# The first loads of a planned attention-and-MLP kernel: slot 0 through the hardware queue, slot 1 cast on chip, decay powers on Pool, and a new plan

## The chip, the cores and the metric

The kernel runs on one core of a Trainium2 chip. Its time is the device time in microseconds of one execution; lower is better. Three runs of the kernel before gave 208.41, 208.84 and 209.43 us, median 208.84. The profile is that of one execution; its times are in us from the start of its span, and an instruction carries the line of the kernel before, such as L614. Engines: PE is TensorE, PEld its weight loads, DVE is VectorE, ACT is ScalarE, POOL is GpSimd, SP is SyncE, which here only issues transfers.

## The reference

Inputs are q, k, v of shape (4, 8, 768, 64) in f32 (batch, heads, time, head dimension) and two MLP weights, `w_in` (512 x 2048) and `w_out` (2048 x 512).

```python
gamma = 1.0 - 2.0 ** (-5.0 - np.arange(H))
for t in range(S):
    state = gamma * state + einsum('bhd,bhe->bhde', k[:, :, t], v[:, :, t])
    y[:, :, t] = scale * einsum('bhd,bhde->bhe', q[:, :, t], state)
# y, transposed to (B*S, H*D), is x
h = x @ w_in
out = (h * np.cos(h)) @ w_out
```

The first part is a recurrent attention with one decay per head; the second is an MLP whose activation is h cos h.

## The kernel before

**Tiles.** Time is cut into chunks of 128, and two batches go together, so there are 12 *slots* (two batch pairs of six chunks). `ORDER` takes the first chunk of both pairs first, so that slots 0 and 1 need no carried state. A slot has 256 rows of x (two batches of 128). Two slots make a *group* of 512 rows, on which the MLP works.

**Steps of a slot p**, by the names that the planner gives them (u and b are halves):

- loads of q, k, v (`load`, L284 to L300), 512 KB of f32 each;
- `cq`, `ck`, `cv`: conversion to bf16 in SBUF (`conv_q`, `conv_k`, `conv_v`). From slot 2 on q and v are multiplied by powers of the decay (`gq`, `gk`) on the way. In slots 0 and 1 the decay lies in the masks `dec` instead, so q and k are only cast, and `rv` makes an undecayed bf16 copy of v (`raw_v`);
- `tq`, `tk` (or `t`): transposes on TensorE (L364), evicted by `eq`, `ek` (L316 on ACT, L318 on DVE). Slots 6 and up are transposed by DMA instead (`dt`, L353);
- `a`: scores (L402 in slots 0 and 1, L392 later), multiplied by the mask in `m` (L411, DVE). For two tiles, one each in slots 0 and 1, ACT saves the scores (`ms`, L419) and Pool multiplies them (`ml`, L423);
- `y`: the output of the slot (L434 in slots 0 and 1, `y_block` with L483, L497, L511 later), and `s`: the state update; `yc` writes y as bf16 into `xt`, the transposed x of the group; `sc` copies the state.

**Steps of the MLP.** A unit of 128 columns of w_in: `f` for a whole group (L593: four matmuls of 512 rows), or `h` for one slot and two column blocks at once (L614: eight matmuls of 256 rows, so that the first slot can start before its neighbour is there). Each is followed by `cos` (L601, ACT) and `mul` (L605 or L622, DVE) into `gt`. `o` is a quarter of an output block (L638), `oc` its copy out of PSUM and its store. h0.0 is the first half unit, on slot 0 with column blocks 0 and 1.

**Order.** The schedule is manual. The opening and the first two groups (slots 0 to 5, and the transposes and scores of slot 6) are ordered by `Plan`: every step has engines, a cost, the steps it comes after, a rank and tokens that it takes (PSUM banks, `cos` buffers, DMA semaphores, one `port` for DVE and Pool steps that read SBUF). `Plan.run` walks through time and gives each free engine its lowest-ranked step that is ready; `SHIFT` changes the ranks of named steps and `ON` their engines. Only the order is kept: each engine executes its list strictly in order, with waits on semaphores for real dependencies. Where TensorE has nothing ready early on, the planner puts in *fillers* (`idle_mm`, L667), matmuls of zeros; seven more stand ahead of the plan. From group 2 on, the order is written out in a loop (the last one of the kernel): there one `f` unit and one `o` part alternate. It begins with `o_mm(1, 0, 0)` and `f_mm(2, 0)`.

**Loads.** Pool issues the software queue in the order of `LOADS`, at most eight in flight: after a first casting load of slot 0's k ("K", f32 in HBM, bf16 in SBUF) come "Q1" and "K1", q and k of slot 1, also cast by the transfer, into `qs` and `kx`; then v0, v1 (f32), and w_in in pieces cast to bf16: w0A (column block 0), w0B (block 1), w0b (2 and 3), w1a, w1b, w2 and so on, with later slots and w_out (`o0` to `o3`) between. SP issues q of slot 0 in two halves ahead of everything (`q0`, `q1` in the call at the start stand for the two batches, not for slots).

Of the kernel before, what the change touches and what calls it, by code (L numbers as in the profile page):

```python
# [28 lines left out]
class Plan:  # L29
# [35 lines left out]
    def run(self, start, cold_until=0.0, look=0.0, fill=None, hold=""):  # L65
# [6 lines left out]
        t = 0.0  # L72
        while left:
            nxt = []
            for e in "SPADE":
# [6 lines left out]
                for op in left:  # L82
# [12 lines left out]
                    for k, n in op["take"]:  # L95
                        tk = sorted(self.tokens[k])
                        n += op["spare"] if k == "bank" else 0
                        if len(tk) < n:
                            ok = False
                            continue  # L100

                        at = max(tk[n - 1] - 0.5, tk[n - 3]) if n > 5 else tk[n - 1]
                        if at > t + 1e-9:
                            nxt.append(at)
                            ok = False
# [33 lines left out]
                for k, n in op["take"]:  # L139
                    self.tokens[k].sort()  # L140
                    del self.tokens[k][:n]
                op.update(eng=e, start=t, free=t + busy, done=t + took, lat=self.LAT[e])
                free[e] = t + busy
                if op["mb"]:
                    self.dma = max(self.dma, t + busy + 1.6) + op["mb"] / op["rate"] + op["lag"]
                    op.update(done=self.dma + 0.9, lat=0.0)
                for k, n in op["give"]:
                    self.tokens[k] += [op["done"] + 0.052] * n
# [18 lines left out]
HOLD = ""  # L167
SHIFT = {"ml010": 25.5, "mulf0.2": -74.7, "f0.3": 0.3, "cosf0.2": -11.6, "cosf0.3": -2.2, "mulf0.3": -4.9, "f0.2": 2.8, "m011": -20.0, "mulh1.4": -20.5, "m000": 82.7, "cosf0.5": -41.6, "ck21": 45.1, "a31": -124.5, "m100": 2.2, "f0.5": 23.0, "a5": -2.5, "v0": -97.2, "ms110": 6.4, "ml110": -41.8, "cosf0.4": -0.9, "f0.4": -9.8, "mulf0.5": 16.9, "eq51": 13.1, "m110": 64.4, "t20": -21.1, "k5": -46.0, "mulf0.8": 31.6, "yc21": -50.4, "f0.6": 2.1, "f0.7": 55.3, "ek10": -92.1, "w0b": -22.2, "a21": -34.2, "h1.0": 81.4, "cosh2.2": 3.0, "m501": 38.5, "yc30": -23.3, "ml011": -27.8, "mulf0.15": 5.8, "sc5": 79.1, "m201": -81.3, "mulh2.2": -18.0, "oc1": -45.8, "mulf0.14": -66.8, "cq31": -32.2, "mulf0.9": -47.9, "mulf0.6": 5.7, "cosf0.7": -27.8, "a30": -8.1, "cosf0.6": -7.2, "h0.2": -12.1, "eq21": -4.6, "cq51": 3.2, "cq41": 38.6, "f0.14": 23.8, "ek20": -13.4, "yc50": 39.8, "cv51": 23.4, "ek51": 88.5, "mulh2.10": 23.3, "cq70": 8.6, "f0.10": -46.0, "mulf0.13": 1.5, "h1.6": 5.9, "ml100": 20.1, "f0.15": 60.8, "o2.1": -8.1, "h3.10": 31.9, "t51": 14.8, "h3.0": -7.1, "h3.14": 28.8, "cq00": -2.7, "m601": 4.7, "h1.4": 1.8, "eq11": 37.0, "cosf0.12": -60.7, "v6": -26.4, "m400": 17.7, "mulh3.12": 67.0, "w2": 49.4, "sw": -53.6, "cv10": -0.0, "rv00": 14.5, "mulh2.8": 4.5, "ek50": 72.2, "cosf0.11": 2.4, "m101": -34.4, "h2.2": 1.1, "q2": -22.9, "q5": -59.7, "cosh3.14": 19.9, "y3": 19.8, "t40": 30.7, "o2": -0.8, "mulh3.4": -0.3, "cq40": -13.2, "mulh0.2": -29.3, "y5": -35.7, "mulh3.14": -25.5, "h2.12": -50.9, "oc0": -94.2, "a10": 39.9, "ek11": -35.3, "h0.6": 6.9, "eq40": -6.2, "h2.6": 58.1, "rv10": -9.1, "dt71": -1.3, "cosh3.8": -31.0, "cosh0.2": 18.8, "cv70": -67.6, "o3.1": -13.8, "cq60": -11.1, "ck60": 71.1, "m511": 10.9, "sc4": -15.9, "o1.3": -16.8, "m510": 4.5, "k4": 12.5, "h0.4": -9.2, "cq71": 3.6, "mulh3.2": 58.9, "cosh1.2": -26.7, "mulh3.6": -1.4, "cv61": 13.7, "o2.2": -9.8, "q6": -7.4, "o0.2": -7.5, "mulh2.4": 44.5, "mulh2.6": 22.6, "mulh3.10": 16.6, "v5": -53.7, "cq61": 27.8, "o1.1": -27.2, "ck61": 0.2, "m200": -10.8, "cosf0.9": 6.3, "cosh0.4": 11.6, "q4": 78.9, "cosh3.6": -6.8, "h1.2": -87.9, "tq01": 1.8, "oc3": -74.8, "mulh0.0": -16.9, "eq01": 11.2, "t21": 6.2, "ck41": 29.7, "cosh3.4": 9.3, "oc2": 8.6, "m211": 23.9, "cq01": -56.9, "w0a": 17.8, "o1.0": -7.7, "yc01": 2.2, "k7": 54.8, "yc51": -0.7, "cosf0.13": -14.9, "cosh2.10": -36.4, "yc00": 7.1, "cosh1.4": -13.4, "ek00": -8.7, "m611": -13.9, "tk10": -101.4, "mulh0.4": -40.7, "mulf0.10": 15.2, "m600": -35.2, "a00": -17.4, "cosh2.0": -5.5, "m301": 18.6, "rv11": -50.0, "sc0": -52.0, "ek01": -31.6, "cv01": 13.3, "ek21": -3.2, "cosf0.10": 7.2, "v7": -2.1, "ek40": 18.1, "t31": 22.7, "mulh1.6": 0.2, "eq30": -9.4, "y4": 19.2, "tk11": 1.9, "ek31": -26.9, "w3b": 23.5, "cosh2.12": -0.2, "cosh0.6": 4.7, "cosh2.8": -4.4, "cosh3.2": 25.8, "cv60": 2.7, "cosh2.4": -14.4, "v4": -1.1, "mulh2.12": 36.6, "dt61": -8.8, "eq41": -12.5, "mulf0.11": 31.8, "ek41": -0.8, "eq50": 9.1, "a11": -23.9, "yc10": 9.3, "o0.3": 0.3, "dt60": -3.3, "o3.3": 50.5, "mulh2.14": -42.3, "m610": -12.1, "f0.11": -0.6, "s0": 3.1, "cv11": 38.9, "h3.8": -17.4, "yc40": 14.3, "m410": -8.4, "h2.8": -4.0, "m300": 15.8, "o0": -14.6, "cv31": -27.4, "rv01": 0.6, "cosf0.14": 2.4, "cosh2.6": 11.7, "cv50": -6.8, "m010": -1.2, "ms011": -12.0, "f0.13": -5.2, "l8": 5.1, "ck70": 3.2, "t41": 1.0, "o1.2": -2.3, "cv71": 0.5, "tq11": 31.2, "h2.4": -3.6, "mulh0.6": 8.8, "t50": 7.1, "ck31": 42.7, "yc20": -52.3, "m001": -4.7, "y01": 62.0, "y2": 15.3, "f0.12": 20.5, "ms111": 2.0, "mulh1.2": -13.9, "cosh3.10": -49.0, "ck51": -9.0, "h0.0": -0.1, "eq31": 1.4, "eq20": -5.1, "q7": 1.5, "cosh3.0": 6.2, "cosh3.12": 1.5, "cv40": 2.3, "y11": 3.6, "o1": -24.4, "cv00": -1.4, "sc2": -3.2, "m411": 18.0, "m210": -8.1, "v3": 0.0, "eq10": 1.1, "tk01": 22.8, "yc41": -25.6, "cq21": -1.8, "f0.9": -31.4}
ON = {"cv70": "P", "cv00": "D", "cv30": "D", "cv31": "D", "cv60": "D", "cv11": "D", "cv10": "P", "rv01": "D", "sc5": "D", "rv11": "A", "yc20": "D", "sc3": "D", "eq40": "DA", "eq50": "A", "rv00": "A", "yc00": "D", "yc31": "DA", "ek51": "D", "ek11": "DA", "sc4": "D", "ek20": "A", "cv61": "P", "eq01": "DA", "cv51": "D", "ek41": "D", "eq41": "A", "cv20": "P", "yc01": "DA", "eq20": "A", "eq30": "DA", "ek50": "D", "ek00": "D", "sc2": "DA", "yc50": "DA", "yc40": "A", "yc21": "A", "cq21": "D", "ek40": "DA", "cv01": "D", "cv71": "P", "cv21": "P", "ek21": "DA", "cv41": "P", "cq20": "D", "ek10": "DA", "yc30": "A", "ek01": "D"}
# [4 lines left out]
def kernel(  # L174
# [170 lines left out]
    def conv_k(p, b, e):  # L345
        copy(e, kb(p)[:, b], kf[p % PRE][:, b])
# [332 lines left out]
    load(nc.sync, 0, "q0 q1")  # L679
    load(nc.gpsimd, 0, "K")  # L680
# [320 lines left out]
```

## Time and profile before

| what | value |
|---|---|
| median of 3 runs | 208.84 us (208.41 to 209.43) |
| profiled execution | span 206.6 us, from its first to its last instruction; the page has no other time of it |
| median less span | 2.24 us |
| PE busy | 201.9 us, 98% of the span |
| PEld, DVE, ACT, POOL busy | 108.9, 112.9, 115.1, 75.2 us |
| fillers (L667) | 35, 11.2 us busy, the last at 17.29 us |
| granted TensorE clock | 9 of 10 or more in all 40 slices |
| software queue | 15408 packets, 15.47 MB |
| hardware queue | 44080 packets, 16.28 MB |

How to read it: a matmul is pipelined, so that PE can be shown busy all the time without being at its peak. What counts is in which order and from when the real matmuls follow one another. The chain that ended last tells which waits decided; the timeline of the opening tells what each first matmul waited for. The start and the length of a transfer's row are those of its issue; "to landing" is the time from the start of the issue until its semaphore.

### The profile page before, as it was taken

The numbers are of one execution on the slowest core, as the hardware profiler recorded it, in microseconds if no ns is written. First come the engines' busy times: TensorE is split into PE (matmuls) and PEld (weight loads), VectorE is DVE, ScalarE is ACT, GpSimd is POOL, SyncE is SP. The second block draws the span as 40 slices with busy tenths as digits, with TensorE's granted clock in tenths as the row PEclk, the third lists the DMA queues.
The fourth block names the chain that finished last, engine by engine and source line by source line (L and its number), as shares of the span: only waits on it lengthen the run. The fifth ranks groups of instructions, "written<-read, shape, count | busy, mean of one in ns | idle before, by whom it ended". The sixth has DMA issues, their size and how long they took to land.

```text
span 206.6 us, 5235 instructions
## 1 busy us (share of the span) xinstructions
PE 201.9 (98%) x2179; PEld 108.9 (53%) x2179; DVE 112.9 (55%) x194; ACT 115.1 (56%) x193; POOL 75.2 (36%) x79
## 2 busy tenths in 40 slices
PE   7999999999999999999999999999999999999994
PEld 2547665868945545445445445445444444444442
DVE  5477899776787548338438438448442444444000
ACT  7566794859965357547547546554555553554120
POOL 8899989799985003305206105200000000000000
PEclk9999999999999999999999999999999999999999
DMA  6999999999999865886876975501101101110212
GB/s 117 172 264 201 304 242 322 252 333 278 341 332 190 199 156 150 206 210 155 190 183 157 144 198 147 156 0 56 53 1 51 51 3 51 51 51 0 105 52 102
DMA packets 59656, 32.15 MB, mean 156 GB/s; under 512 B 48752, under 2 KB 54128, under 8 KB 59632
## 3 DMA queue, kind: packets, MB, share of 16 engines
q0 software_dynamic: 15408, 15.47, 34.6%
q1 hardware_dynamic: 44080, 16.28, 31.7%
q8 instruction: 17, 0.28, 0.6%
q10 hardware_dynamic: 144, 0.07, 0.1%
q14 instruction: 7, 0.06, 0.1%
HBM read 27.26 MB, written 6.29 MB: 162 GB/s over the span
## 4 chain that ended last, share of the span: by engine, by line
PE 93%; DMA 4%; POOL 1%; issue 0%; DVE 0%; POOLq 0%; DVEq 0%
PE bank L638 39%; PE bank L593 30%; PE bank L614 10%; DMA kx<-in_k_dram 4%; PE bank L392 2%; PE bank L483 2%; PE bank L364 2%; PE bank L658 2%; PE st_ps L511 2%; PE bank L667 2%; PE bank L497 1%; POOL ks L284 1%; PE bank L434 1%; POOL qs L284 1%; PE bank L402 0%
## 5 line engine op out<-in xcount | busy, mean ns | idle before, releaser
L601 ACT ACTIVATE cosb<-bank,halfpi 128x512 bf16<-128x512 f32 x96 | 65.6, 689 | 54.1 <-PE bank L593 47.8
L638 PE MATMUL bank<-w_out_sb,gt 128*128 128x512 bf16 x368 | 91.0, 379 | 0.0
L605 DVE TENSOR_TENSOR gt<-bank,cosb 128x512 bf16<-128x512 f32 x72 | 49.1, 689 | 55.7 <-ACT cosb L601 55.7
L593 PE MATMUL bank<-xt,w_in_sb 128*128 128x512 bf16 x288 | 73.2, 379 | 0.0
L638 PEld LDWEIGHTS <-gt 128*128 128x128 bf16 x368 | 35.5, 98 | 42.3 <-DMA w_out_sb<-in_moe_w_out_dram 0.3
L593 PEld LDWEIGHTS <-w_in_sb 128*128 128x128 bf16 x288 | 27.5, 98 | 32.3
L327 POOL TENSOR_TENSOR qs<-qf,gq 128x512 bf16<-128x512 f32 x18 | 18.5, 1046 | 42.4 <-PE bank L483 32.0
L411 DVE TENSOR_TENSOR am<-bank,mask 128x512 bf16<-128x512 f32 x40 | 24.8, 681 | 3.5 <-PE bank L392 3.5
L316 ACT COPY ob<-bank 128x512 f32<-128x512 f32 (+1 forms) x24 | 14.0, 582 | 16.0 <-PE bank L638 13.9
L614 PE MATMUL bank<-xt,w_in_sb 128*128 128x256 bf16 x192 | 22.4, 273 | 0.0
L614 PEld LDWEIGHTS <-w_in_sb 128*128 128x128 bf16 x192 | 18.6, 98 | 3.3 <-DVE xt L318 0.3
L622 DVE TENSOR_TENSOR gt<-bank,cosb 128x512 bf16<-128x512 f32 x24 | 16.2, 689 | 5.6 <-ACT cosb L601 5.4
L316 ACT CAST xt<-bank 128x512 bf16<-128x512 f32 x21 | 11.4, 588 | 10.6 <-PE bank L483 10.5
L316 ACT CAST ks<-kf 128x512 bf16<-128x512 f32 x20 | 11.5, 623 | 1.9 <-DMA kf<-in_k_dram 1.9
L667 PE MATMUL bank<-zero 128*128 128x512 bf16 x35 | 11.2, 449 | 1.1 <-DVE halfpi L683 1.1
L483 PE MATMUL bank<-am,vs 64*64 64x128 bf16 (+1 forms) x320 | 10.3, 206 | 0.1
L334 POOL TENSOR_TENSOR vs<-vf,gk 128x512 bf16<-128x512 f32 x8 | 8.2, 1043 | 6.0 <-DMA vf<-in_v_dram 3.8
L284 POOL DMA_DIRECT2D vf<-in_v_dram x8 | 9.4, 1178 | 1.9 <-DVE vs L339 1.4
L339 POOL TENSOR_TENSOR vs<-vf,gk 128x512 bf16<-128x512 f32 x8 | 8.7, 1096 | 2.5 <-PE bank L483 1.3
L318 DVE CAST stb<-st_ps 128x512 bf16<-128x512 f32 x9 | 6.2, 689 | 3.4 <-PE st_ps L511 2.6
L483 PEld LDWEIGHTS <-vs 64*64 64x64 bf16 x320 | 7.8, 107 | 0.5 <-POOLq L531 0.2
L392 PE MATMUL bank<-qkt 64*64 64x128 bf16 (+1 forms) x320 | 7.9, 206 | 0.0
(66 smaller groups left out, 131.7 us busy)
## 6 DMA issues: line engine op xcount, KB each, us to landing
out_dram<-ob SPq DMA_DIRECT2D x23, 256.0 KB, 2.5
vf<-in_v_dram POOLq DMA_DIRECT2D x8, 512.0 KB, 11.7
qf<-in_q_dram POOLq DMA_DIRECT2D x6, 512.0 KB, 12.3
kf<-in_k_dram POOLq DMA_DIRECT2D x6, 512.0 KB, 12.1
w_out_sb<-in_moe_w_out_dram POOLq DMA_DIRECT2D x4, 512.0 KB, 14.1
qf<-in_q_dram SPq DMA_DIRECT2D x4, 512.0 KB, 4.8
w_in_sb<-in_moe_w_in_dram POOLq DMA_DIRECT2D x5, 256.0 KB, 8.5
kf<-in_k_dram SPq DMA_DIRECT2D x16, 64.0 KB, 3.1
```

What stands on the lines that cost most here:

```text
L284: eng.dma_start(out=t.rearrange("p b h d -> p (b h) d"), in_=src[ds(2 * bp, 2), :, ds(c * C, C), :].rearrange("b h t d -> t (b h) d"))
L316: nc.scalar.copy(out=out, in_=in_)
L327: ENG[e].tensor_tensor(out=qb(p)[:, b], in0=qf[p % PRE][:, b], in1=bc(gq, ORDER[p] % NC), op=ALU.mult)
L411: nc.vector.tensor_tensor(out=am[p % 2][b][u], in0=bank.rearrange("p (a t) -> p a t", a=HP), in1=(dec[:, b] if p < 2 else mask[second(p, 0 ...
L483: m = nc.tensor.matmul(held["yp", p][b][ts(j, 64), a, lo:], lhsT=vs[p % NB][ts(r, 64), b, h, :], rhs=am[p % 2][b][h // 4][ts(r, 64), h % 4 ...
L593: nc.tensor.matmul(bank, lhsT=w_in_sb[:, i, ts(f, 128)], rhs=xt[g % 2][:, i, :], start=(i == 0), stop=(i == KIN - 1))
L601: nc.scalar.activation(out=cb, in_=bank, func=AF.Sin, bias=halfpi)
L605: nc.vector.tensor_tensor(out=gt[g % 2][:, f, :], in0=bank, in1=cb, op=ALU.mult)
L614: nc.tensor.matmul(bank[:, ts(e, 256)], lhsT=w_in_sb[:, i, ts(f + e, 128)], rhs=xt[g % 2][:, i, ts(hf, 256)], start=(i == 0 and e == 0), s ...
L622: nc.vector.tensor_tensor(out=gt[g % 2][:, f : f + 2, ts(hf, 256)], in0=bank.rearrange("p (f t) -> p f t", f=2), in1=cb.rearrange("p (f t) ...
L638: nc.tensor.matmul(bank, lhsT=gt[g % 2][:, f, ts(j, 128)], rhs=w_out_sb[:, f, :], start=(f == 0), stop=(f == KOUT - 1))
L667: nc.tensor.matmul(bank[:, : 256 * n].rearrange("p (n t) -> p n t", n=n), lhsT=zero[:, :128], rhs=zero.unsqueeze(1).to_broadcast([128, n, ...
```

## The change

- SP loads q and k of slot 0, each as two halves, in the order q, k, q, k. The casting load of slot 0's k on Pool's queue goes.
- Slot 0's k is therefore f32 in SBUF and is cast by a `ck` step. Slot 1's q and k ("q1", "k1" in `LOADS`) are loaded as f32 into `qf` and `kf` and cast by `cq` and `ck` steps, on DVE or ACT.
- The eight products that make `lgp` (the exponents of the decay powers) move from DVE to Pool; behind them Pool fills `ob[3]` with zeros and copies it to `ob[2]`. Both are output buffers that are overwritten before their first use. All of this stands ahead of Pool's first load.
- In `Plan`, a step on ACT no longer takes the `port` token; the rates, delays and starting times that the planner reckons with are others; `yc` of slots 0 and 1 and `rv` may go to DVE or ACT.
- `SHIFT` and `ON` are new, so the order of nearly all steps of the plan is another. Fillers in the plan: 24 where there were 28. Instructions: 190 rows of DVE where there were 185, 179 of ACT (175), 73 of Pool (70).

```diff
-    load(nc.sync, 0, "q0 q1")
-    load(nc.gpsimd, 0, "K")
+    load(nc.sync, 0, "q0 k0 q1 k1")
...
     for h in range(H):
-        nc.vector.tensor_scalar(out=lgp[:, :, h], in0=pos, scalar1=float(lg[h]),
+        nc.gpsimd.tensor_scalar(out=lgp[:, :, h], in0=pos, scalar1=float(lg[h]),
                                 scalar2=None, op0=ALU.mult)
+    nc.gpsimd.memset(ob[3], 0.0)
+    for i in range(1):
+        nc.gpsimd.tensor_copy(out=ob[2 - i], in_=ob[3])
...
-    LOADS = ["Q1", "K1", "v0", "v1", "w0A", "w0B", "w0b", "w1a", "w1b", "w2", "q2", ...]
+    LOADS = ["q1", "k1", "v0", "v1", "w0A", "w0B", "w0b", "w1a", "w1b", "w2", "q2", ...]
...
-            if p == 1:
-                T["cq", p, b], T["ck", p, b] = ld["q", p, b], ld["k", p, b]
+            if p == 1 and "Q1" in LOADS:
+                T["cq", p, b] = ld["q", p, b]
             else:
-                T["cq", p, b] = add("D" if p < 2 else CQ if p < 3 else "P", SB2 if p < 2 else TT,
+                T["cq", p, b] = add("DAP" if p < 2 else CQ if p < 3 else "P", SB3 if p < 2 else TT,
...
-            if p == 0:
+            if p == 1 and "K1" in LOADS:
                 T["ck", p, b] = ld["k", p, b]
-            elif p > 1:
-                T["ck", p, b] = add("A", SB2, lambda e, p=p, b=b: conv_k(p, b, e),
+            else:
+                T["ck", p, b] = add("DAP" if p < 2 else "A", SB3, lambda e, p=p, b=b: conv_k(p, b, e),
...
-            T["yc", p, b] = add("A", PS, lambda e, p=p, b=b: y_copy(p, b, e),
+            T["yc", p, b] = add("DA" if p < 2 else "A", PS, lambda e, p=p, b=b: y_copy(p, b, e),
...
                 for k, n in op["take"]:
+                    if k == "port" and e == "A":
+                        continue
```

The order that comes out of it at the places that matter (compiled, without times):

```
PE before:   ... tk10 tk11 3 fillers a11 a10 2 fillers y01 y00 7 fillers h0.0 y10 y11 filler h0.2 s0 h1.2 h0.4 h1.4
PE changed:  ... tk11 filler tk10 filler a11 filler y00 y01 a10 3 fillers h0.0 y10 y11 filler h0.2 h1.2 h1.4 s0
end before:  ... o3.1 o3.2 y5 o3.3 | o_mm(1,0,0) f_mm(2,0)
end changed: ... o2.2 o3.3 o2.3 y5 | o_mm(1,0,0) f_mm(2,0)
ACT changed: ... cq01 ck01 ek00 ek01 eq11 ms011 ck11 ck10 ek11 rv00 ms111 yc00 yc01 rv11 cosh0.0
DVE changed: cq00 ck00 eq00 eq01 cq11 m010 cq10 m001 eq10 m000 ek10 rv01 m101 rv10 m110 m100 cv01 yc11
POOL changed: lgp x8, fill, copy, q1 k1 v0 v1 w0A w0B w0b ml011 w1a w1b w2 ml111 q2 k2 w3a v2
```

## The prediction

> **What bounds the kernel now.** I read the page first (busy time, then the chain that ended last), then the chain in order of time, then the timeline of the opening.
>
> ```profile
> span 206.6 us, 5235 instructions
> PE 201.9 (98%) x2179; PEld 108.9 (53%) x2179; DVE 112.9 (55%) x194; ACT 115.1 (56%) x193; POOL 75.2 (36%) x79
> PE 93%; DMA 4%; POOL 1%; issue 0%; DVE 0%; POOLq 0%; DVEq 0%
> ```
>
> TensorE holds 93% of the chain; what is left lies at the start. In order of time (start, length, what):
>
> ```profile
> 1.42 1.37 POOL ks L284
> 2.79 1.13 POOL qs L284
> 3.93 7.40 DMA kx<-in_k_dram
> 14.30 1.62 PE bank L667 x7
> 15.91 0.87 PE bank L614 x8
> ...
> 69.69 1.83 PE bank L638 x8
> 71.52 1.73 PE bank L593 x8
> ```
>
> The chain begins with Pool issuing three casting loads, goes through the landing of slot 1's k at 3.93 + 7.40 = 11.33, through fillers (L667), and from 15.9 stays on real matmuls. The timeline shows what the first real one had waited for:
>
> ```profile
> 4.74 0.60 DVE L318 CAST qs<-qf 128x512 bf16<-128x512 f32 x1 [0.51 <-DMA qf<-in_q_dram]
> 5.06 2.35 POOL L284 DMA_DIRECT2D vf<-in_v_dram  x2
> 7.35 2.31 POOL L303 DMA_DIRECT2D w_in_sb<-in_moe_w_in_dram  x3
> ...
> 12.97 0.62 ACT L316 CAST gt<-vf 128x512 bf16<-128x512 f32 x1 [0.58 <-DMA vf<-in_v_dram]
> 13.66 0.64 PE L434 MATMUL bank<-am,gt 128*64 128x128 bf16 x16
> 14.11 0.59 ACT L316 CAST xt<-bank 128x512 bf16<-128x512 f32 x1
> 14.23 1.69 PE L667 MATMUL bank<-zero 128*128 128x512 bf16 x7
> 14.51 0.68 DVE L318 CAST xt<-bank 128x512 bf16<-128x512 f32 x1
> 15.75 1.04 PE L614 MATMUL bank<-xt,w_in_sb 128*128 128x256 bf16 x8
> ```
>
> h0.0 (L614) starts at 15.75. Its xt is ready at 15.19; w0A landed at 7.35 + 7.9 = 15.25 and w0B at 8.10 + 7.8 = 15.9 (their rows of issue to landing). Those follow v0 in one software stream, and v0's landing (5.06 + 7.9 = 12.95) is what the casts at 12.97 waited for. From 15.75 to the first unit of the hand-written part (L593 at 71.36) pass 55.6 us. The work in it: 24 half units at 0.873, 8 full at 0.864, 17 output parts at 0.864, 8 transpose groups at 0.44, three score groups at 0.57, y blocks 2 x 1.33 + 2 x 1.48, and 1.15 for y10, y11, s0 and one filler: 54.5. So 1.1 us are waits and switches, and the stage is a block that slides with its start. After 71.36 the code is unchanged: 135.2 us.
>
> **The change part by part.**
> *Hardware queue.* Slot 0's q halves, issued at 0.74 and 1.27, landed at 3.77 and 4.72: 0.95 us per half. With q0 k0 q1 k1 the landings are about 3.8, 4.7, 5.7, 6.6 (k landed at 1.42 + 6.3 = 7.7). SP issues two DMAs more, at 0.55 each, before its next one (L901 at 5.22): 1.1 us in an idle queue. k needs two casts more, on DVE (0.43) and ScalarE (0.6), q's second half one on ScalarE instead of DVE. ScalarE is bound there by its table load and sine, until 6.71; then two casts to 7.9, transposes to 8.4, and scores near 8.8, where L402 stands now (8.78). Nothing won or lost.
>
> *Pool's head.* One casting load goes; ahead of the first load come eight products for the decay powers, a fill and a copy, each of 128x512 f32 for the latter two. Pool's iotas end at 1.16. The eight products: 0.67 on DVE today; Pool's iotas are 0.13 to 0.15 each, so 0.67 to 1.2; I take 0.8. Fill and copy: a cast of that shape is 0.43 on DVE, a two-input product on Pool 1.04; so 0.86 to 2.1 together, and I take 1.0, nearer to the low end, since neither reads two tensors. The first software load (q1) is thus issued at 3.0, between 2.7 and 4.5, where Q1 was issued at 2.79.
>
> *The stream.* K, issued at 1.42, landed 6.3 later; in the windows from 5 to 9 us the chip moved 134 to 154 GB/s of cast output, and 347 to 353 from 10 to 12 us in f32. K, Q and K1 landed at 7.7, 9.4, 11.3 (1.8 apart), v0 and v1 1.6 apart, w0A and w0B 0.7. An issue takes 1.17. Afterwards q1 begins to flow some 2.4 after its issue starts, at 5.4, but has the hardware queue beside it until about 6.0; its 1.6 of transfer and 1.2 to the semaphore give 8.6 (without sharing 8.2; at an issue of 4.5, 9.7). Then k1 10.2, v0 11.8, v1 13.4, w0A 14.05, w0B 14.8, w0b 16.1: each 1.1 to 1.2 earlier than now. The queue gains one cast load (1.8) and 0.2 on each of two; it loses 0.9 to the later start.
>
> By the Trainium skill, SBUF — State Buffer, § SBUF: two separate sides, a VectorE copy in a two-port mode locks GpSimd out of writing descriptors. The casts at 3.80 and 4.74 lay beside the issues of 2.79 to 5.06, which kept 1.17 each, and the second cast took 0.60 instead of 0.43: here VectorE paid. By the rule q1's issue would lose 0.43 for each of two casts, and the sum 0.9 of its gain; by the rows nothing.
>
> *Casts of slot 1.* Four new ones (ck11, ck10 on ScalarE, cq11, cq10 on DVE) stand between landing and transposes. q1 is early: hidden. k1 lands at 10.2: ck11 to 10.8, ck10 to 11.4, tk11 beside it, ek11 (ScalarE) to 12.0, then rv00 to 12.6 (v0 came at 11.8). DVE's ek10 and rv01 end by 12.8. So the y matmuls run 12.7 to 13.3 (13.66 to 14.3 now). ms111 is ahead of both yc on ScalarE: to 13.2; yc00 to 13.75, yc01 to 14.3 (both on ScalarE now, 0.55 apart; today one is on DVE). a10 and three fillers end at 14.2. xt at 14.3, w0A at 14.05, w0B needed at 14.9: h0.0 at 14.45, 1.3 earlier. The casts cost 0.6 after k1, covered by waiting for v0; if v0 came earlier, they would be the path.
>
> *Behind h0.0.* The same matmuls in another order. y11 needs ml111, a Pool product behind ten loads and ml011: four issues of 1.17 and six of 0.76 from 3.0, with ml011 (1.27, held to 10.35 by ms011) among them, put it at 13.9 to 15.2 (14.16 to 15.4 now), needed at 15.6. Pool's issue order is late by 0.2 to 0.7, hidden as loads land 8 us after issue. w0b at 16.1, needed at 16.2; w1a 17.9, needed 18.0: no slack, they go with the stream. The wait for o0 ahead of o1.0 and its neighbours (L638, 0.28 of idle PEld) goes with an earlier stream: 0.15 won.
>
> *The end of the stage.* Today o3.3 stands after y5; in the change y5 is the last planned matmul, and only o_mm(1,0,0), 0.87, lies between it and the first full unit, which needs both yc5. Today ScalarE casts them at 69.73 for 1.07, just behind y5's end at 69.69. So the unit waits 0.04 + 1.07 + 0.1 - 0.87 = 0.34. This is a new wait; o3.3 hid it.
>
> *Edits of one answer.* Four fillers fewer, all ahead of h0.0, and the planner's numbers cost nothing by themselves; the clock was 1.00 in every window.
>
> Sum: -1.3 - 0.15 + 0.34 = -1.1 us: span 205.5. The page has no time of the profiled execution but its span; 2.24 lie between it and the median of 208.84 (runs 208.41 to 209.43), and I leave these as they are: 207.7.
>
> **The rivals.**
> *The gain is mostly eaten* (0 to 1 us, 208.3). If Pool's first load is issued at 3.6 to 4.0, or the three ScalarE steps ahead of yc run 0.3 late, h0.0 starts at 15.0 to 15.5. For it: the bounds of Pool's new work, and no slack at w0b and w1a. Against it: the k1 path alone would not reach beyond 14.9.
>
> *Slower: Pool's head starts the stream too late.* The landings move one for one with q1's issue. Gain is zero at an issue of 4.1; beyond 5.2 the kernel is slower by 0.5%. That needs the eight products, the fill and the copy to take 4 us in place of 1.8, and gives, at 5.5, w0B at 17.3, h0.0 at 16.95: 1.2 + 0.2 later, 210.2. For it: Pool's K issue, beside DVE's start-up work, took 1.37 in place of 1.17, and that work is still beside it. Against it: even at the upper bounds the issue is at 4.5.
>
> *A first use that stalls.* Three kinds of Pool instruction run for the first time ahead of the first load. Pool's first product (L423 at 10.18) took 1.27 and its second (14.16) 1.27 as well: a first call cost nothing there. Should one of the new kinds stall for 5 us, q1 would be issued at 8.0 and the kernel, one for one, end at 212.7; as no row shows such a stall I give it 2%. By the Trainium skill, GPSIMD Engine Reference, § 2.1 Instruction dispatch, the first call of a freshly loaded kernel pays about 6 us; the two rows of 1.27 do not show that for the product.
>
> **How the numbers follow.** A measurement of this kernel tells about 0.5% (1.04 us) from no change. Forecast (206.9 to 207.8): 46%, faster. Eaten gain: 33%, same. Slower: 21%, of which 19% by a late stream and 2% by the stall. The likeliest gives 207.7. The low end of the range is the forecast with an issue at 2.7 and a little over half of the other waits gone, 206.9 (4% below it); the high end is the late stream at an issue of 5.4, 210.1 (16% above it). The forecast's own range is the one beside its chance.
>
> **What would show it.** After: Pool's first load at 2.7 to 3.3; q1 landing near 8.6 and v0's casts near 11.9; h0.0 near 14.5; the last planned matmul y5 followed by one output part and then an idle stretch of TensorE of about 0.3 before the first full unit. The first unit of the hand-written part stands at 70.2 and 135.2 follow. I am wrong if Pool's head ends after 4.1, if h0.0 waits for xt rather than for weights beyond 15, or if TensorE shows idle time above 0.5 us between h0.0 and the end of the plan.

## The result, and the profile after

The changed kernel takes 211.48 us (median of 4 runs, 211.09 to 212.81) where the kernel before takes 209.02 in the same rounds. The ratio is 1.0129, with a 95% interval from 1.0093 to 1.0165. The forecast was 207.7, with 210.1 as the high end of its range: the change is slower by 2.5 us, not faster by 1.1. Every ratio below is worked out from all executions in the same rounds except those that fell in a slower state (one each of e1 and e6), so it is not the ratio of the two medians beside it.

The profiled execution has a span of 209.5 us (206.6 before) and a time of its own of 211.22. Lines of the changed kernel lie 8 below those of the kernel before: L622 is h0.0's line (L614 before), L601 the full units', L646 the output parts', L326 and L324 the casts and copies of DVE and ACT, L347 and L335 the products of `conv_v` and `conv_q`, L431 the Pool product `ml`. First the page: span, busy time of the engines, and the shares of the chain that ended last.

```profile
span 209.5 us, 5212 instructions
PE 201.0 (96%) x2151; PEld 109.5 (52%) x2175; DVE 115.2 (55%) x192; ACT 115.8 (55%) x193; POOL 78.5 (37%) x88
PE 88%; DVE 4%; DMA 3%; issue 2%; POOL 2%; ACT 1%; POOLq 0%; DVEq 0%
```

TensorE holds 88% of the chain in place of 93%, and VectorE, which had no share, has 4%. The chain in order of time (start, length, what) tells where:

```profile
2.14 1.11 POOL lgp L702 x5
4.83 5.66 DMA qf<-in_q_dram
...
17.72 0.89 PE bank L622 x8
...
40.10 1.30 DVE vs L347
...
73.83 1.89 PE bank L601 x8
```

The chain now begins with the decay powers on Pool and goes through q1, the first software load, in place of slot 1's k. Far behind the opening, at 40.10, stands a VectorE product of 1.30 us, which before took 0.69. The timeline of Pool gives its head:

```profile
1.26 2.29 POOL L702 TENSOR_SCALAR lgp<-pos 128x6 f32<-128x6 f32 x8
3.61 0.53 POOL L704 MEMSET ob<- 128x512 f32 x1
4.20 0.68 POOL L706 COPY ob<-ob 128x512 f32<-128x512 f32 x1
4.83 1.35 POOL L292 DMA_DIRECT2D qf<-in_q_dram  x1
```

The eight products on 128x6 numbers take 2.3 us, more than the fill and the copy together. The first software load is issued at 4.83. The timeline of the opening, and of the stretch near 40 us:

```profile
10.51 0.43 DVE L326 CAST qs<-qf 128x512 bf16<-128x512 f32 x1 [2.27 <-DMA qf<-in_q_dram]
10.99 0.40 PE L372 MATMUL bank<-ident,qs 128*128 128x128 bf16 x4 [1.67 <-DVE qs L326]
...
17.58 1.03 PE L622 MATMUL bank<-xt,w_in_sb 128*128 128x256 bf16 x8
...
39.78 1.05 POOL L335 TENSOR_TENSOR qs<-qf,gq 128x512 bf16<-128x512 f32 x1
40.10 1.30 DVE L347 TENSOR_TENSOR vs<-vf,gk 128x512 bf16<-128x512 f32 x1
```

VectorE waited 2.27 for q1 and TensorE 1.67 behind it. h0.0 starts at 17.58 (15.75 before). The product at 40.10 lies beside a product of Pool. The windows by stretch (start:end, us, busy time of PE, PEld, DVE, ACT and POOL, granted clock, share of the DMA engines, GB/s) add one thing:

```profile
8.00:10.00 2.00, 1.32 (x15) 0.62 (x13) 0.24 (x1) 0.81 (x2) 2.00 (x3) 1.00 0.98 319
10.00:12.00 2.00, 1.01 (x15) 0.62 (x16) 1.49 (x4) 0.57 (x2) 2.00 (x3) 1.00 1.01 318
12.00:14.00 2.00, 2.00 (x13) 1.05 (x13) 1.40 (x3) 1.67 (x5) 1.59 (x3) 0.60 1.05 344
14.00:16.00 2.00, 2.00 (x16) 0.92 (x15) 1.12 (x3) 1.25 (x3) 2.00 (x3) 0.55 1.62 191
```

The last two of these windows in the kernel before:

```profile
12.00:14.00 2.00, 2.00 (x33) 1.00 (x33) 1.45 (x4) 1.42 (x3) 1.70 (x3) 1.00 1.30 251
14.00:16.00 2.00, 2.00 (x22) 1.06 (x17) 2.00 (x4) 1.70 (x4) 1.84 (x2) 1.00 1.59 190
```

Behind a stretch in which TensorE was busy for 2.33 of 4 us, its granted clock falls to 0.60 and 0.55 in two windows that were at 1.00 before. The 2.9 us of the span divide so: h0.0 is 1.83 late; the stage behind it, up to the first unit of the hand-written part (73.83 against 71.36), is 0.64 longer; the hand-written part is 0.09 longer up to its last full unit; and 0.30 lie behind that unit, where the last store is issued 2.9 us ahead of the end in place of 2.6. These 0.3 are in the profiles of the changed kernel and of every variant of it, and not in those of the two variants of the kernel before (e3, e7); why, stays open.

### The profile page after: what moved, and what is told of

Same layout as the page of the kernel before. It is cut to its first block, busy times and chain, and to the rows that moved or that the text cites. A ratio compares the mean times of both kernels' runs of the same rounds, so it can differ in the third digit from the quotient of the medians.

```text
span 209.5 us, 5212 instructions
## 1 busy us (share of the span) xinstructions
PE 201.0 (96%) x2151; PEld 109.5 (52%) x2175; DVE 115.2 (55%) x192; ACT 115.8 (55%) x193; POOL 78.5 (37%) x88
## 4 chain that ended last, share of the span: by engine, by line
PE 88%; DVE 4%; DMA 3%; issue 2%; POOL 2%; ACT 1%; POOLq 0%; DVEq 0%
PE bank L646 37%; PE bank L601 29%; PE bank L622 8%; DMA qf<-in_q_dram 3%; PE bank L400 2%; PE bank L491 2%; PE bank L372 2%; PE bank L675 2%; PE bank L666 2%; PE st_ps L519 2%; PE bank L505 1%; DVE gt L630 1%; POOL lgp L702 1%; DVE vs L347 1%; DVE am L419 1%
## 5 line engine op out<-in xcount | busy, mean ns | idle before, releaser
L646 PE MATMUL bank<-w_out_sb,gt 128*128 128x512 bf16 x358 | 90.0, 379 | 1.1 <-issue 0.5
L601 PE MATMUL bank<-xt,w_in_sb 128*128 128x512 bf16 x274 | 71.1, 379 | 0.6 <-issue 0.2
L646 PEld LDWEIGHTS <-gt 128*128 128x128 bf16 x368 | 35.6, 98 | 41.8
L601 PEld LDWEIGHTS <-w_in_sb 128*128 128x128 bf16 x288 | 27.6, 98 | 32.4 <-issue 0.3
L335 POOL TENSOR_TENSOR qs<-qf,gq 128x512 bf16<-128x512 f32 x18 | 19.3, 1086 | 42.8 <-PE bank L491 41.6
L324 ACT COPY ob<-bank 128x512 f32<-128x512 f32 (+1 forms) x24 | 13.9, 581 | 16.8 <-PE bank L646 14.6
L622 PE MATMUL bank<-xt,w_in_sb 128*128 128x256 bf16 x192 | 22.6, 273 | 0.1
L622 PEld LDWEIGHTS <-w_in_sb 128*128 128x128 bf16 x192 | 18.6, 98 | 3.9 <-DVE xt L326 0.3
L324 ACT CAST xt<-bank 128x512 bf16<-128x512 f32 x22 | 12.0, 588 | 9.0 <-PE bank L491 8.9
L324 ACT CAST ks<-kf 128x512 bf16<-128x512 f32 x21 | 12.2, 623 | 0.5 <-DMA kf<-in_k_dram 0.5
L347 POOL TENSOR_TENSOR vs<-vf,gk 128x512 bf16<-128x512 f32 x8 | 8.7, 1103 | 1.9 <-DMA vf<-in_v_dram 1.8
L326 DVE CAST stb<-st_ps 128x512 bf16<-128x512 f32 x9 | 6.2, 688 | 4.5 <-PE st_ps L519 4.5
L292 POOL DMA_DIRECT2D kf<-in_k_dram x7 | 8.3, 1188 | 0.4 <-DVE gt L613 0.4
L292 POOL DMA_DIRECT2D qf<-in_q_dram x7 | 8.4, 1207 | 0.0
```

Of the source, the lines that this page charges most:

```text
L292: eng.dma_start(out=t.rearrange("p b h d -> p (b h) d"), in_=src[ds(2 * bp, 2), :, ds(c * C, C), :].rearrange("b h t d -> t (b h) d"))
L324: nc.scalar.copy(out=out, in_=in_)
L335: ENG[e].tensor_tensor(out=qb(p)[:, b], in0=qf[p % PRE][:, b], in1=bc(gq, ORDER[p] % NC), op=ALU.mult)
L601: nc.tensor.matmul(bank, lhsT=w_in_sb[:, i, ts(f, 128)], rhs=xt[g % 2][:, i, :], start=(i == 0), stop=(i == KIN - 1))
L622: nc.tensor.matmul(bank[:, ts(e, 256)], lhsT=w_in_sb[:, i, ts(f + e, 128)], rhs=xt[g % 2][:, i, ts(hf, 256)], start=(i == 0 and e == 0), s ...
L646: nc.tensor.matmul(bank, lhsT=gt[g % 2][:, f, ts(j, 128)], rhs=w_out_sb[:, f, :], start=(f == 0), stop=(f == KOUT - 1))
```

## The experiments

Each time below is a median, with its ratio to the kernel before in the same rounds and the 95% interval of that ratio. "f(2,1)" is the start of the weight load of the second unit of the hand-written part, which shows what the opening and the planned part cost together: 72.01 before, 74.47 in the changed kernel.

**Is it the powers, or the fill and the copy?** Two runs undo one part of Pool's head each.

```diff
 # e1: the eight powers on VectorE again
-        nc.gpsimd.tensor_scalar(out=lgp[:, :, h], in0=pos, ...
+        nc.vector.tensor_scalar(out=lgp[:, :, h], in0=pos, ...
 # e2: no fill, no copy
-    nc.gpsimd.memset(ob[3], 0.0)
-    for i in range(1):
-        nc.gpsimd.tensor_copy(out=ob[2 - i], in_=ob[3])
```

> The changed kernel with one part undone: the eight products for the decay powers are back on DVE; Pool's fill and copy stay. Theory A (the opening: Pool's head of 3.6 us holds back the software stream, and the rest follows): Pool's first load moves from 4.83 to about 2.5, the stream then shares the chip with the hardware queue until 6, v0 lands near 11.8 instead of 13.8, h0.0 starts near 14.6 instead of 17.6, TensorE has no half-clock stretch, and the median falls by 2.5 to 3 us to 208.5 to 209.0. Rival B (the new order of the plan is slower by itself, with DVE as the bound between 40 and 48 us): h0.0 moves, but most of it is lost again behind it; 210.5 or more.

> The changed kernel without Pool's fill and copy (they hold nothing that the output needs); the eight products stay on Pool. Theory A: Pool's first load at 3.6 instead of 4.83; landings 1.2 earlier, h0.0 at 16.0 to 16.4, the gap of TensorE near 9 to 11 us shorter by 1.2 and with it perhaps no half-clock stretch; 209.5 to 210.2. Rival B: 211 or more. If the time follows the first load one for one, this run and the one with the products on DVE lie on one line of slope 1.

e1 took 213.52 (1.0189, 1.0132 to 1.0246), e2 211.65 (1.0130, 1.0074 to 1.0187). Neither won anything, although the first load went out at 2.31 and 3.60, so an early start alone was no gain. Why e1 lost still more stays open: its one profile is of its slowest execution (216.14; the other three took 211.91 to 214.01), and what that one shows need not hold for them. e2 shows more. Its h0.0 starts at 15.57, 0.18 ahead of the kernel before, and yet f(2,1) is at 74.49. The timeline of e2:

```profile
14.87 2.01 DVE L326 CAST gt<-vf 128x512 bf16<-128x512 f32 x1 [0.26 <-DMA vf<-in_v_dram]
15.29 1.29 POOL L431 TENSOR_TENSOR am<-gt 128x512 bf16<-128x512 f32 x1
...
18.13 0.64 PE L442 MATMUL bank<-am,gt 128*64 128x128 bf16 x16 [1.44 <-DVE am L419]
```

The cast is `rv10`, slot 1's first undecayed half of v. It takes 2.01 us beside `ml`, Pool's product. In the changed kernel the same cast takes 0.42, and there Pool's product is the longer one, 1.52 in place of 1.27:

```profile
16.36 0.42 DVE L326 CAST gt<-vf 128x512 bf16<-128x512 f32 x1
16.39 1.52 POOL L431 TENSOR_TENSOR am<-gt 128x512 bf16<-128x512 f32 x1 [0.30 <-ACT gt L427]
```

In e2 TensorE stands idle 1.44 us ahead of 18.13, for the masks that VectorE makes behind this cast. Its weight loads wait 1.19 more ahead of 30.69, behind products of slot 2's q at 26.17 (1.49) and 29.38 (1.26) that lie beside products of Pool as well.

**The powers alone, in the kernel before.**

```diff
-    load(nc.gpsimd, 0, "K")
...
-        nc.vector.tensor_scalar(out=lgp[:, :, h], in0=pos, ...
+        nc.gpsimd.tensor_scalar(out=lgp[:, :, h], in0=pos, ...
...
+    load(nc.gpsimd, 0, "K")
```

> The kernel before with one part of the change alone: its eight products for the decay powers on Pool, ahead of the first casting load. Theory A: K is issued at 3.6 instead of 1.42, every landing 2.2 later, TensorE idles where it waits for k of slot 0, h0.0 near 17.9; 211 to 212. Rival B: the old order has room, since fillers stand there; 209 to 209.5.

210.56 (1.0080, 1.0050 to 1.0109). Timeline of Pool in e3:

```profile
1.25 2.29 POOL L694 TENSOR_SCALAR lgp<-pos 128x6 f32<-128x6 f32 x8
3.60 1.34 POOL L284 DMA_DIRECT2D ks<-in_k_dram  x1
```

The load is issued 2.18 later than before (1.42). h0.0 comes 1.45 later, f(2,1) 2.10, and the median is 1.6 longer. So a late start of the stream is paid in the old order as well, at 0.7 of its size, and the powers' 2.3 us have nothing to do with the new plan.

**The clock.** Seven more matmuls of zeros ahead of the transposes that wait for q1 keep TensorE busy.

```diff
 def t_mm(p, u, w):
+        if (p, u, w) == (1, 1, 0):
+            for i in range(7):
+                nc.tensor.matmul(banks.free_list[0][:, :]..., lhsT=zero[:, :128], ...)
```

> The changed kernel with seven more fillers in TensorE's list just ahead of the first transposes of slot 1's q, where it idled for 1.7 us in the profile and where the granted clock fell to 0.60 and 0.55 in the two windows behind. Theory A1 (the half-clock stretch is a part of the loss): the clock stays at 1.00, scores and y matmuls of slots 0 and 1 take half as long, h0.0 near 16.7 instead of 17.58; 210.4 to 210.8. Rival A2 (landings alone set h0.0): the clock stays, h0.0 does not move, 211.4.

212.83 (1.0182, 1.0128 to 1.0237), outside both expectations. The granted clock stayed at 1.00 and h0.0 moved from 17.58 to 16.31, so the half clock did delay it, by about a microsecond. But f(2,1) is at 76.09, 1.6 later than without the fillers. Timeline of e4:

```profile
15.56 2.01 DVE L326 CAST gt<-vf 128x512 bf16<-128x512 f32 x1 [0.24 <-DMA vf<-in_v_dram]
15.99 1.29 POOL L437 TENSOR_TENSOR am<-gt 128x512 bf16<-128x512 f32 x1
```

The same cast, the same 2.01. An earlier opening brings it beside Pool's product, and TensorE's weight loads then wait 1.09, 1.27 and 0.98 (ahead of 18.82, 31.46 and 46.73), each time for VectorE. The changed kernel's own four runs hint at the same: the two with a mean clock of 1.00 took 211.74 and 212.81, the two with 0.992 took 211.22 and 211.09.

**The cast off VectorE.** The first half of slot 1's `rv` joins the second on ScalarE, behind its two casts of slot 0's y; in e5 the fill and the copy are left out too, in e9 they stay.

```diff
 def raw_v(p, b, e):
+        if (p, b) == (1, 0):
+            return
+        if p == 1:
+            copy("A", vr[p][:, 0], vf[p % PRE][:, 0])
```

> The run without Pool's fill and copy, with one cast moved: the bf16 copy of the first half of slot 1's v (rv10) goes from DVE to ScalarE, behind both yc of slot 0. There it took 2.01 us on DVE beside Pool's product ml111 (15.29 to 16.58) where it takes 0.42 alone, and y11 waited for the masks behind it, 1.2 us. Theory C (DVE and Pool shut each other out of SBUF when the new order lays a conversion on DVE beside a product on Pool, and that holds TensorE): the wait between y10 and y11 goes, the first full unit of the hand-written part moves from 73.45 to 72.3 to 72.6, 210.4 to 210.8. Rival D (landings of weights set the stage behind h0.0): the wait only moves to the next unit, 211.5.

> The changed kernel with one edit: both halves of the first conversion of slot 1's v to bf16 (rv10, which VectorE held and which took 2.01 us beside Pool's product in the run without fill and copy) are made by ScalarE, behind its two casts of slot 0. The eight powers, the fill and the copy stay on Pool, so its first load starts near 4.8 and h0.0 near 17.5. This closes a table of four: changed kernel 211.48, without fill and copy 211.65, without both fill-and-copy and the VectorE conversion 209.46. Theory that losses overlap (the late head and the locked conversion hide each other, since a late start lets Pool's product come after the conversion): here the conversion costs nothing to begin with, and the run stays at 211.2 to 211.8. Rival, losses add: the conversion costs its 2 us in the changed kernel too, and the run falls to 209.5 to 210.2.

e5 took 209.46 (1.0030, 1.0005 to 1.0055), e9 210.52 (1.0084, 1.0052 to 1.0117). With e2 and the changed kernel they make a table of four:

| ratio to before | `rv10` on VectorE | `rv10` on ScalarE |
|---|---|---|
| fill and copy ahead of the loads | 1.0129 | 1.0084 |
| neither | 1.0130 | 1.0030 |

While the cast is on VectorE, taking 1.2 us out of Pool's head shows no gain; with the cast on ScalarE it is worth 0.0054, 1.1 us. In the other direction, the cast costs 0.9 us with the late head and 2.1 with the earlier one. The 2.1 and the 1.1 are clear of the intervals; the 0.9 is not, as 1.0093 to 1.0165 and 1.0052 to 1.0117 overlap. Timeline of e5:

```profile
15.39 1.29 POOL L435 TENSOR_TENSOR am<-gt 128x512 bf16<-128x512 f32 x1
15.50 1.15 ACT L324 CAST gt<-vf 128x512 bf16<-128x512 f32 x2
```

ScalarE's two casts of v take 1.15 together beside the same Pool product. The edit brings back what the kernel before did, as its own timeline shows, with a Pool product at 14.16 beside them:

```profile
14.16 1.27 POOL L423 TENSOR_TENSOR am<-gt 128x512 bf16<-128x512 f32 x1 [0.46 <-ACT gt L419]
14.60 1.14 ACT L316 CAST gt<-vf 128x512 bf16<-128x512 f32 x2
```

For e9 neither expectation held: the theory said that the cast cost nothing there, and the median fell by 1.0; the rival said 2. In e9's profile h0.0 stands where it did (17.59) and f(2,1) is at 74.05. The cast had taken only 0.42 in the changed kernel's profile, so what its move won there is elsewhere, at the product of 40 us. Pool's product still lies beside it, but now begins behind it, and Pool's is the one that grows. Timeline of e9:

```profile
40.11 0.68 DVE L347 TENSOR_TENSOR vs<-vf,gk 128x512 bf16<-128x512 f32 x1
40.16 1.53 POOL L335 TENSOR_TENSOR qs<-qf,gq 128x512 bf16<-128x512 f32 x1
```

In the changed kernel Pool's had begun 0.32 ahead (39.78), and VectorE's took 1.30. e9's three runs with a mean clock of 0.992 took 210.77, 210.81 and 211.92, the three with 0.998 or 1.00 210.09, 210.24 and 210.26.

> The run with seven extra matmuls on zeros ahead of the product that waits for slot 1's q (clock kept at 1.00, h0.0 1.27 earlier, and yet 212.83), now with the conversion rv10 on ScalarE as well. Theory (the early start was taken back by VectorE's conversion locked beside Pool's product): the conversion no longer takes 2.01, h0.0 stays near 16.3, f(2,0) comes to 72.6 to 73.4 in place of 75.0, and the run ends at 209.9 to 211.0. Rival (the clock at half was only a symptom, and time is lost behind h0.0 whatever VectorE does): 212 to 213.

e10 is e4 with the cast on ScalarE: 210.36 (1.0066, 1.0044 to 1.0088), against 212.83 for e4, as the theory had it. The clock is 1.00, the weight loads of q1's transposes wait 1.20 for it, h0.0 starts at 16.83, and behind 11.44 the matmuls of the planned part stand idle nowhere for more than 0.25. f(2,1) is at 73.29: h0.0 is 1.08 late and f(2,1) 1.28. So this run holds the late stream without the other two losses, and that costs 1.3 us.

**A second conversion moved.** `cv10`, the decayed half of slot 1's v, is made by Pool just ahead of the load of slot 6's v; otherwise as e5.

```diff
-            o = add("P", 1.2, lambda e, ...: load(nc.gpsimd, p, n),
+            o = add("P", 1.2, lambda e, ...: (conv_v(1, 0, "P", True) if (n, p) == ("v", 6) else None, load(nc.gpsimd, p, n)),
```

> The same, and Pool's product of the undecayed first half of slot 1's v with the powers (cv10, not needed before slot 6) stands just ahead of slot 6's load of v instead of beside DVE's conversions of slot 2's q, which took 1.49 and 1.26 in place of 0.68 while t20 waited 1.07 us for them. Theory C: 0.7 to 1.1 us less than with rv10 alone, 209.4 to 210.0, no longer clearly slower than the kernel before. Rival D: the same time as with rv10 alone.

209.99 (1.0090, 1.0047 to 1.0134), not better than e5. TensorE's weight loads wait 0.74 ahead of 32.91, for w_out, and 0.89 ahead of 55.58, for a product of Pool. Its ten runs fall into two lots, six from 209.54 to 210.05 and four from 212.37 to 212.84; what decides between them stays open. The expectation that moving this product would win as well was wrong.

**One collision in the kernel before.** Pool makes one more product, of an unused buffer, ahead of the load of slot 3's v.

```diff
+    nc.vector.memset(ob[2], 1.0)
...
-            o = add("P", 1.2, lambda e, ...: load(nc.gpsimd, p, n),
+            o = add("P", 1.2, lambda e, ...: (nc.gpsimd.tensor_tensor(out=ob[3], in0=ob[2], in1=ob[2], op=ALU.mult) if (n, p) == ("v", 3) else None, load(nc.gpsimd, p, n)),
```

> The kernel before with one product on Pool added (on an output buffer, its result is not used) ahead of slot 3's load of v, near 24.6 us, where DVE converts slot 2's q (L327 at 24.76, 0.68 now). Theory C: that conversion takes 1.2 to 1.7, t20 and everything behind it moves by 0.5 to 0.9 us; 209.4 to 209.9. Rival D, and also if the old order has slack there: the conversion grows and the time stays at 209.0.

208.81 (1.0000, 0.9982 to 1.0017). Timeline of e7:

```profile
24.16 1.08 POOL L729 TENSOR_TENSOR ob<-ob 128x512 f32<-128x512 f32 x1
24.27 1.53 DVE L327 TENSOR_TENSOR qs<-qf,gq 128x512 bf16<-128x512 f32 x1
26.92 0.67 DVE L327 TENSOR_TENSOR qs<-qf,gq 128x512 bf16<-128x512 f32 x1
```

The price of a collision can be seen by itself: 1.53 beside Pool, 0.67 alone, and the two work on different buffers. From h0.0 to f(2,1) e7's profile has 56.53 us against 56.26 in the kernel before, and the weight loads of the scores at 30.11 wait 0.75 for VectorE in place of 0.50. The median shows no loss, within some 0.4. So a collision has no fixed price for the kernel: this one was nearly covered in the old order, where the one of `rv10` in e2 and e4 stands ahead of a matmul for which TensorE waits.

**The stream at the issue time that was assumed.** The powers are back on VectorE, and a second copy keeps Pool's first load at 2.87, where the prediction had it at 3.0. e8 has both conversions moved, as in e6; e11 has `rv10` on ScalarE alone.

```diff
-        nc.gpsimd.tensor_scalar(out=lgp[:, :, h], in0=pos, ...
+        nc.vector.tensor_scalar(out=lgp[:, :, h], in0=pos, ...
...
-    for i in range(1):
+    for i in range(2):
         nc.gpsimd.tensor_copy(out=ob[2 - i], in_=ob[3])
```

> The changed kernel with the eight products on DVE, the fill and two copies on Pool, so that its first load is issued near 3.0 as the prediction had assumed, and with rv10 and cv10 moved as in the run with two removed. By the prediction's step on the stream: q1 lands at 8.6, v0 at 11.8, w0B at 14.8, h0.0 at 14.5, and with the collisions gone 207.7 to 208.3. Rival E (the early software stream only takes from the hardware queue: with an issue at 2.31 the last half of slot 0's k finished at about 10 us, and at 3.60 v0 landed at 13.2): v0 at 12.9 to 13.2 or slot 0's k late, h0.0 at 15.4 or later, 209.4 or more.

> The changed kernel with Pool's first load at 2.9 (the eight powers on VectorE, the fill and two copies on Pool), which is the issue time that the prediction assumed, and with rv10 on ScalarE; the earlier run at this issue had a second conversion moved as well, and ended at 212.15 with new waits at 39.1, 54.4 and 62.4. If those waits came of the second conversion's move: h0.0 near 15.3, f(2,0) 70.9 to 71.6, 208.8 to 209.8, that is no better than before by more than 0.2. The prediction's own step (landings 1.1 earlier, gain 1.1): h0.0 14.5 and 207.7. Rival (an early start meets another collision on VectorE, at slot 2's q or slot 3's v): f(2,0) beyond 72.5 and 210.5 to 212.5.

e8 took 212.15 (1.0119, 1.0059 to 1.0179; three of its four runs at 212.09 to 212.54, one at 209.68), e11 208.91 (0.9998, 0.9978 to 1.0017), as its first expectation had it. Here is what the first load's issue did to the landings, from the profiles:

| kernel | q1 issued | q1 | k1 | v0 | w0B | h0.0 |
|---|---|---|---|---|---|---|
| predicted | 3.0 | 8.6 | 10.2 | 11.8 | 14.8 | 14.45 |
| e8 | 2.87 | 9.27 | 11.15 | 12.89 | 15.96 | 15.28 |
| e11 | 2.87 | by 8.96 | by 11.14 | 12.06 | 15.33 | 15.13 |
| e2 | 3.60 | 9.59 | 11.44 | 13.22 | 16.04 | 15.57 |
| changed | 4.83 | 10.49 | 12.09 | 13.79 | 16.68 | 17.58 |
| before | 2.79 | 9.43 | 11.32 | 12.95 | 15.95 | 15.75 |
| e7 | 2.72 | 8.89 | 10.61 | 12.17 | 15.43 | 15.26 |

(In e11 the two landings are not in the trace; the times are the starts of the casts that need them.)

e7 has the opening of the kernel before, and its landings came 0.5 to 0.8 earlier than in that kernel's own profile; e8 and e11 share an opening too and differ by 0.6 and 0.8. So one row against another tells no more than that. Taken together, w0B lands at 15.33 and 15.96 with the issue at 2.87, at 15.43 and 15.95 in the order before, and at 16.68 to 17.30 in the four profiles with the issue at 4.8 (the changed kernel, e4, e9, e10). At the assumed issue it is no earlier than before, and the predicted 14.8 was reached nowhere. In e8 TensorE's weight loads wait 1.06 ahead of 40.98 and 0.90 ahead of 55.89 for products of Pool, and its matmuls stand idle 1.42 ahead of 64.03. These waits are gone in e11, which differs from it by the place of `cv10` alone: that move brought them. In the answer on the tile `vs` of e8 from 30 to 66 us (count, shortest, median and longest in ns) its longest conversion on VectorE stands out:

```profile
L349 POOL TENSOR_TENSOR vs<-vf,gk x7: 1032/1044/1057, 29.0 to 65.5; 128x512 bf16<-128x512 f32 x7
L349 DVE TENSOR_TENSOR vs<-vf,gk x3: 693/1083/3317, 38.6 to 60.1; 128x512 bf16<-128x512 f32 x3
```

One took 3.32 us, near 60, beside three products of Pool in a row, while none of Pool's in this stretch took more than 1.06. e11 is the best form of the change that was run, and it equals the kernel before. It began h0.0 0.62 earlier than the kernel before (0.13 earlier than e7), but its f(2,1) is at 72.16, no earlier. Timeline of e11:

```profile
11.34 1.28 POOL L435 TENSOR_TENSOR am<-gt 128x512 bf16<-128x512 f32 x1 [1.48 <-ACT gt L431]
12.57 2.29 POOL L311 DMA_DIRECT2D w_in_sb<-in_moe_w_in_dram  x3
...
19.05 1.05 PE L626 MATMUL bank<-xt,w_in_sb 128*128 128x256 bf16 x8 [0.25 <-DMA w_in_sb<-in_moe_w_in_dram]
```

Pool waits 1.48 for ScalarE's scores, multiplies, and issues w1a at 12.57 (11.40 before). It lands at 19.01 (19.07 before), and TensorE, for whom it should have come earlier, waits 0.5.

## Why the prediction was wrong, step by step

Term by term, the sum had h0.0 at -1.3, and it was +1.83; the stage behind it at -0.15, and it was +0.45; the new wait at its end at +0.34, and it was +0.19.

**Pool's head: too small.** The step took 0.8 for the eight products and 1.0 for fill and copy. They took 2.35 from start to start, 0.29 each, and 1.22. The first load was issued at 4.83, beyond the upper bound of 4.5. Fill and copy were inside their bounds; the products were not, since an iota was no row for what Pool pays for a product. This is the first step that failed. With the cast on ScalarE, the late head as a whole costs 1.8 us (e9 to e11): leaving out fill and copy is 1.1 of it (e9 to e5), and putting the powers back with the issue held at 2.87 is 0.7 (e5 to e11, where the intervals still overlap).

**The stream: wrong even at its own issue time.** "Each 1.1 to 1.2 earlier than now" was worked out as one cast load less in the queue. At 2.87, 0.13 ahead of the assumed issue, w0B landed 0.5 (e11) and 1.2 (e8) later than predicted, on average where it did before (15.65 against 15.69). An issue 1.96 earlier than the changed kernel's made w0B only some 1.3 earlier, mean to mean. A likely cause is that slot 0's k was not removed, only moved to the hardware queue, whose transfers share the DMA engines with the software queue's; the 0.2 that the step charged for sharing was then far too small. The windows fit this (here the one from 6 to 7 us, first of the changed kernel, then of e11): with the late issue the DMA engines are nearly free in it, with the early one their share stays between 0.98 and 1.30 from 2 to 12 us.

```profile
6.00:7.00 1.00, 1.00 (x10) 0.53 (x8) 0.00 (x0) 0.99 (x3) 1.00 (x2) 1.00 0.25 51
6.00:7.00 1.00, 1.00 (x8) 0.58 (x8) 0.00 (x0) 1.00 (x1) 1.00 (x2) 1.00 1.05 259
```

No run takes slot 0's k off both queues, so this cause is argued and not shown. What is shown is that the assumed head does not give the gain: e11 has it, without the collision of `rv10`, and equals the kernel before. That the hardware queue lands its halves "near 3.8, 4.7, 5.7, 6.6" held nearly: the casts of the first two start at 3.74 and 4.63, the third landed at 5.63, and the fourth, which the trace of the changed kernel does not tell, at 6.92 in e11.

**Casts of slot 1 and h0.0: the clock was left out.** The step had h0.0 at 14.45, which with a head 1.83 later would be 16.28. e10, in which neither the clock falls nor the cast collides, has 16.83; e4, with the clock kept too, 16.31. So the path from q1 to h0.0 was about right, and q1's lateness is worth some 0.6 to 1.1 on h0.0. In e11 the condition that the step named came true, that slot 1's casts are the path once v0 is early: v0 landed at 12.06, but its cast on ScalarE began at 12.74, behind the two casts of slot 1's k and a copy. The profile of the changed kernel has 0.75 more than e10: the clock, which "was 1.00 in every window" of the kernel before and fell here behind the wait for q1. Seven more fillers in that wait kept it up (e4, e10). The prediction named the four fillers that went and priced their loss at nothing, without asking what keeps the clock up if a load is late. The 1.00 of the very first windows cannot be taken at its word either: seven fillers at 1.06 took 3.17 us, seven at 14.23 took 1.69. In e9's runs the drop is worth about 0.6. By the Trainium skill, TensorE: Matmul & The Clock Gate, § What's actually happening, the clock is halved after an idle window of about 3.4 us. The length agrees: the two windows at 0.60 and 0.55 hold 1.6 + 1.8 = 3.4 us at half. The condition is weaker here, as TensorE was busy for more than half of the 4 us before. This section of the Trainium skill also says that the window runs free and does not start with the kernel; that some executions of a kernel show the drop and others don't would fit this, but no run here shows the window.

**Behind h0.0: the stage was no block that slides.** The step held that the same matmuls in another order take the same time, less 0.15. They took 0.45 more up to the last planned part, and all of it lies behind the product at 40.10, beside Pool's. The half unit ahead of that product's reader (43.77; 41.93 before) stands 26.19 behind h0.0, against 26.18 before; the next one stands 29.90 behind h0.0 (47.48), against 29.45 before (45.20). In e9, where the product took 0.68, it is 29.46. And where the opening starts earlier, other collisions take its place: waits of 1.4 and 1.2 in e2, three of about 1 in e4. This is the mechanism that no part of the prediction had, and it turns every repair of the opening alone into nothing (e2) or a loss (e4).

**VectorE and Pool: the row misled, the rule warned.** The prediction weighed a rule of the Trainium skill, SBUF — State Buffer, § SBUF: two separate sides, and set it aside, since Pool's issues beside VectorE's casts kept their 1.17. The same section of the Trainium skill calls the shared pair of ports an exclusive lock, between a Pool operation and a VectorE operation in a two-port mode or, where Pool reads SBUF, of two SBUF inputs. The runs agree on that: 0.68 became 1.30 in the changed kernel and 1.53 in e7, 0.42 became 2.01 in e2 and e4, and TensorE's wait behind that cast went away with its move to ScalarE (e5, e10). The cast had been on ScalarE before and was put on VectorE by the new plan, which the order in the section on the change shows and which I did not price. I had looked for Pool's loss at its DMA issues, and the loss was VectorE's, beside Pool's products. The planner's `port` token is meant to keep the two apart, but it does so by the planner's clock, in which Pool begins at 3.6; in the profile Pool's first load came at 4.83.

**The tail: right, a little less.** A new wait of 0.34 was predicted between y5 and the first full unit; ScalarE's two casts stand at 72.70, the output part at 72.77 and the unit at 73.83, where 73.64 was possible: 0.19.

**Span and median: 0.43 off.** The 2.24 between span and median were kept. The profiled execution of the changed kernel has 211.22 - 209.5 = 1.72 between its own span and its own time; in the other variants, too, 1.7 to 1.8 lie between. For the kernel before that makes 208.4, the lowest of its three runs; its profiled execution lay 0.4 below the median, and the step carried that on.

Of the rivals, "Pool's head starts the stream too late" came nearest: right in place and sign. Its price was not: its rule gives 0.7 us of loss at 4.83, and 2.5 were measured. What is shown of these 2.5 comes from one edit after the other: the cast off VectorE 0.9 (changed kernel to e9), fill and copy 1.1 (to e5), the earlier issue with the powers on VectorE 0.7 (to e11), and then nothing is left. The amounts hold for this order of removal alone, as the table of four shows, and the first and the last are not clear of the intervals one by one; that the three together remove the loss is.

## What to carry to other kernels

A load moved to another queue is not gone: take the gain from measured landings at a given issue time, over more than one execution, and not from the length of the queue. When one planned order is replaced by another, list the VectorE operations that lie beside Pool's elementwise work, because each may take two to five times its length (0.68 became 1.30, 0.42 became 2.01) and the plan's own clock does not keep them apart once a start slips. And a repair that wins nothing may be half of one: taking the fill and the copy out of Pool's head won nothing alone, moving the cast off VectorE 0.9 us, and the two together 2.1.

## What the runs showed of the hardware that I had not expected

- A product of 128x6 numbers took Pool 0.29 us, eight of them 2.29; VectorE did the eight in 0.67. Size is not what sets this: a fill of 128x512, 85 times as many numbers, took Pool 0.53, a copy 0.68.
- Beside a Pool product of 1.29, VectorE's cast of 128x512 from f32 to bf16 took 2.01 in place of 0.42 (e2, e4). That is more than waiting for the product to end, and it is so though the cast's row begins 0.42 ahead of the product's. In the changed kernel the two rows begin 0.03 apart, the cast first, and there Pool pays (1.52 in place of 1.27), as at 40.11 in e9 (1.53 in place of 1.05). The section of the Trainium skill cited above says that who starts first holds the ports. These two pairs agree, and so does 40.10 in the changed kernel, where Pool began first and VectorE paid; e2 and e4 do not. In both of them Pool was issuing loads until its product began, and whether that counts as a start no run here shows.
- ScalarE's casts of the same shape took 1.14 and 1.15 for two beside a Pool product, 0.62 for one with none: no slowing beside Pool is seen.
- An idle stretch of TensorE of 1.67 us in the changed kernel and of 1.71 in e9 was followed by 3.4 us at half the clock in the profiles; stretches of 0.98 (e2) and 1.06 (e5) were not. Of the changed kernel's four executions, two show the drop in their mean clock (0.992) and two do not (1.00).
